# A fused attention and ELU layer on one core: batch 1 turned earlier, the second layer begun earlier, loads moved up

## The chip, the cores and the metric

One core of a Trainium2 chip runs the whole kernel. The metric is the device time in microseconds (us) of one execution; lower is better. Three runs of the kernel before gave 333.58, 333.91 and 334.61 us, with a median of 333.91 us.

## What is computed

```python
# q, k, v: (8 batches, 8 heads, 576 positions, 64), float32
scores = q @ k.T / 8                                   # per batch and head
scores = where(0 <= i - j < 128, scores - slope[h] * |i - j|, -1e9)
attn   = exp(scores - max) / (sum(exp(scores - max)) + 1e-9)
x      = (attn @ v)  laid out as (8 * 576 = 4608 tokens, 8 * 64 = 512)
h      = x @ w_in                                      # 512 -> 2048
g      = where(h > 0, h, exp(min(h, 0)) - 1)           # ELU
out    = g @ w_out                                     # 2048 -> 512, float32
```

A query sees only the 128 positions up to its own, so for each block of 128 keys only 256 queries matter. The 4608 tokens are worked on in nine blocks of 512 by the two layers; a batch has 576 tokens, so token blocks and batches do not line up.

## The kernel before

All matrix work is in float16 on TensorE (PE), with sums in float32 in PSUM. VectorE (DVE), ScalarE (ACT) and GpSimd (POOL) do the rest; POOL also issues the loads. The order of all work is written by hand as a list of slots: in each slot the engines get the pieces below, and each engine runs its own pieces in the order in which they were issued.

The pieces of a slot that matter here:

```python
def hidden(t, c0, w, f0, nf, p):        # first layer: one PSUM bank p of h
    ...                                 # PE: 16 matmuls of 128 columns (32 of 64)
    nc.scalar.activation(e, p, AF.Exp)  # ACT: e = exp(h)
    nc.gpsimd.tensor_scalar(e, e, 1.0, 0.0, min, max)      # POOL

def elu(t, c0, w, f0, nf, p):           # DVE: g = max(e - 1, h); frees the bank p
    V.scalar_tensor_tensor(out=gs[t][...], in0=e, scalar=1.0, in1=p,
                           op0=ALU.subtract, op1=ALU.max)

def output(t, ts, f0, bank=None):       # second layer: 4 of 16 matmuls of 512 columns
    if f0 == 0: ops[t, ts] = bank or ps_o.tile(..., tag="op")
    for fc in range(f0, f0 + 4): nc.tensor.matmul(o, gs[t][...], w_out_sb[...])
    if f0 == 12:
        nc.scalar.copy(ob, o)           # ACT, then SP stores 128 tokens

def values(b, i, part, bank=None):      # attn @ v for four heads of a block of 128 queries
    ...                                 # PE: 4 or 8 matmuls of 65 columns
    V.reciprocal(out=r, in_=a[..., D])  # DVE: rden
    V.tensor_tensor(out=xn, in0=a[..., 0:D], in1=r, op=ALU.mult)    # DVE: xn

def turn(b, i, copy=None, bank=None):   # xn -> xT: 4 PE transposes and a copy, or a DMA

def load_first(b, w, part):             # K (w=1) or Q (w=0) of batch 0 or 1 to SBUF:
    p0, p1 = ((0, 64), (64, 96))[part]  # part 0: positions 0..383, part 1: 384..575
    nc.gpsimd.dma_start(s0[b][p0:p1, w, ...], (q, k)[w][b, :, 6*p0:6*p1, :] ...)

def turn_first(b, w, part, half, bank, copy):   # transposes of that on PE, then one copy
    n, nh = ((64, 2), (32, 4))[part]            # part 0 in two halves of the heads
    for x in range(nh):
        for j in range(6):
            for hh in range(2): nc.tensor.transpose(t[...], s0[b][...], ident[r, r])
    copy(o, t)                                  # PSUM -> QT or KT

def first_scores(b, u, half, d): ...    # PE: q.k of key block u, batches 0 and 1
def first_expo(b, u, half, d, ...): ... # ACT: EX = exp(scores / 8)
def first_weigh(b, u, half): ...        # DVE: EX *= table of slopes and mask
def turn_qk(b, w, h2, dh): ...          # from batch 2 on: K and Q turned on DVE
```

Three banks serve the hidden steps of slots 4 to 17, so the hidden step of slot s can begin only when the `elu` of slot s - 3 has freed its bank:

```python
BUF = [hp[0], hp[1], sp[2], sp[3]]
HID[s if s < 18 else s + 8] = [(*step, BUF[s % 2 if s < 4 else (s + 1) % 3 if s < 18 else (s + 1) % 2])]
...
s = 13 + o if o < 13 else 2 * o + 1 if o < 16 else 17 + o      # slot of second-layer piece o
OUT[s] = (t, ts, 4 * f, sp[3] if t == 0 and ts % 2 else hp[ts - 2] if o >= 16 * NTB - 8 else None)
...
at(6, values, 0, 3, 0); at(6, values, 0, 3, 1, "op")
at(7, turn, 0, 3, nc.scalar.copy)
at(7, values, 0, 4, 0); at(7, values, 0, 4, 1, "op")
at(8, turn, 0, 4, nc.scalar.copy)
```

The loop that issues a slot:

```python
for s in range(min(slots), max(slots) + 1):
    for f, a in early.get(s, []): f(*a)                 # exponentials of earlier scores
    for step in HID.get(s, []): hidden(*step)
    for r in [s - 1] if s < 4 or s > 17 else [] if s == 4 else [s - 2] if s < 17 else [15, 16]:
        for step in HID.get(r, []): elu(*step)
    for f, a in tasks.get(s, []): f(*a)                 # values, turn, scores, loads
    if s in OUT: output(*OUT[s])
```

The first 16 hidden steps are those of token block 0. Slots 18 to 25 have no hidden step: the tokens of the next ones come from batch 1, whose attention is worked out in these slots.

Of the kernel before, what the change touches and what calls it, by code (L numbers as in the profile page):

```python
# [18 lines left out]
def kernel(  # L19
# [9 lines left out]
    nc = tc.nc  # L29
# [4 lines left out]
    NTB = NTOK // 512  # L34
# [3 lines left out]
    V = nc.vector  # L38
# [36 lines left out]
    sp = [spa[:, 0, :], spa[:, 1, :]] + [ps_s.tile([128, 512], F32, name=f"sp{i}", tag=f"sp{i}") for i in (2, 3)]  # L75
    hp = [ps_h.tile([128, 512], F32, name=f"hp{i}", tag=f"hp{i}") for i in range(2)]
# [8 lines left out]
    def load_first(b, w, part):  # L85

        p0, p1 = ((0, 64), (64, 96))[part]
        nc.gpsimd.dma_start(  # L88
            s0[b][p0:p1, w, :, :, :].rearrange("p h j d -> p h (j d)"),
            (q, k)[w][b, :, 6 * p0:6 * p1, :].rearrange("h (p j) d -> p h (j d)", j=6))  # L90
# [8 lines left out]
    def load_v(b, n):  # L99
        p = 128 if n < 4 else 64  # L100
        nc.gpsimd.dma_start(VP[b % 2][0:p, n, :, 0:D],  # L101
                            v[b, :, 128 * n:128 * n + p, :].rearrange("h p d -> p h d"))

    def load_wi(i):
        c = slice(512 * i, 512 * i + 512)
        nc.gpsimd.dma_start(w_in_sb[:, :, c], moe_w_in[:, c].rearrange("(c p) f -> p c f", p=128))
# [31 lines left out]
    with tc.manual_schedule():  # L138
# [104 lines left out]
        def hidden(t, c0, w, f0, nf, p):  # L243
            if p is None:
                p = ps_o.tile([128, 512], F32, name="ho", tag="op")
            hps[t, c0, f0] = p
            a = (512 * t + c0) % RING
            cuts = [(0, w, a)] if a + w <= RING else [(0, RING - a, a), (RING - a, w, 0)]
            for l in range(nf):
                fc = f0 + l  # L250
                for u0, u1, x0 in cuts:
                    for c in range(4):
                        nc.tensor.matmul(  # L253
                            p[:, l * w + u0:l * w + u1], w_in_sb[:, c, fc * 128:(fc + 1) * 128],
                            xT[:, c, x0:x0 + u1 - u0], start=(c == 0), stop=(c == 3))
            e = es[t, c0, f0] = work.tile([128, 512], F32, name="e", tag="e", bufs=6)
            n = w * nf
            nc.scalar.activation(e[:, 0:n], p[:, 0:n], AF.Exp)  # L258
            nc.gpsimd.tensor_scalar(out=e[:, 0:n], in0=e[:, 0:n], scalar1=1.0, scalar2=0.0,  # L259
                                    op0=ALU.min, op1=ALU.max)  # L260

        def elu(t, c0, w, f0, nf, p):
            if t not in gs:
                gs[t] = gpool.tile([128, NFC, 512], F16, name="g", tag="g")
            sh = lambda ap: ap[:, 0:w * nf].rearrange("p (l c) -> p l c", c=w)
            V.scalar_tensor_tensor(  # L266
                out=gs[t][:, f0:f0 + nf, c0:c0 + w], in0=sh(es.pop((t, c0, f0))), scalar=1.0,
                in1=sh(hps.pop((t, c0, f0))), op0=ALU.subtract, op1=ALU.max)

        def output(t, ts, f0, bank=None):  # L270
            if f0 == 0:
                ops[t, ts] = bank if bank is not None else ps_o.tile([128, DO], F32, name="op", tag="op")
            o = ops[t, ts]
            for fc in range(f0, f0 + 4):
                nc.tensor.matmul(o, gs[t][:, fc, ts * 128:(ts + 1) * 128], w_out_sb[:, fc, :],  # L275
                                 start=(fc == 0), stop=(fc == NFC - 1))
            if f0 == 12:
                ob = work.tile([128, DO], F32, name="ob", tag="ob")
                nc.scalar.copy(ob, o)  # L279
                nc.sync.dma_start(out[512 * t + 128 * ts:512 * t + 128 * ts + 128, :], ob)  # L280
# [13 lines left out]
        load_v(0, 0)  # L294
        load_v(0, 1)
        load_first(0, 0, 1)
        load_first(0, 1, 1)
        load_wi(0)
        load_wi(1)
        load_v(0, 2)  # L300
        load_wi(2)
        load_v(0, 3)
# [56 lines left out]
        early, tasks, HID, OUT = {}, {}, {}, {}  # L359

        def at(s, f, *a):
            tasks.setdefault(s, []).append((f, a))

        def before(s, f, *a):
            early.setdefault(s, []).append((f, a))

        BUF = [hp[0], hp[1], sp[2], sp[3]]
# [5 lines left out]
        steps += [(1, 192, 64, 8 * f, 8) for f in range(2)]  # L373
        steps += [(1, c0, 128, 4 * f, 4) for c0 in (256, 384) for f in range(4)]
        for s, step in enumerate(steps):
            HID[s if s < 18 else s + 8] = [(*step, BUF[s % 2 if s < 4 else (s + 1) % 3 if s < 18 else (s + 1) % 2])]
        for t in range(2, NTB):
            for j in range(16):
                step = (128 * (j // 4), 128, 4 * (j % 4), 4) if t < 4 else (256 * (j // 8), 256, 2 * (j % 8), 2)
                HID[16 * t + 8 + j] = [(t, *step, BUF[(j + 1) % 2])]  # L380
        for o in range(16 * NTB):
            t, ts, f = o // 16, o // 4 % 4, o % 4
            s = 13 + o if o < 13 else 2 * o + 1 if o < 16 else 17 + o
            OUT[s] = (t, ts, 4 * f, sp[3] if t == 0 and ts % 2 else hp[ts - 2] if o >= 16 * NTB - 8 else None)


        at(0, values, 0, 1, 0)
# [4 lines left out]
        for half in range(2):  # L392
            at(1, first_scores, 0, 2, half, half)
            for c in range(2):
                before(2 + c, first_expo, 0, 2, half, half, 128 * c, 128 * c + 128)
        at(1, turn_first, 0, 1, 1, 0, None, nc.scalar.copy)
        at(3, values, 0, 2, 0)
        at(3, values, 0, 2, 1, "op")
        at(3, first_scores, 0, 3, 0, 0)
# [15 lines left out]
            at(s, load_wo, 2 + n)  # L415
        at(2, load_first, 1, 1, 0)
        at(3, load_first, 1, 0, 0)
        at(7, load_first, 1, 1, 1)
        at(9, load_first, 1, 0, 1)
        for n, s in enumerate((4, 5, 12, 14, 17)):  # L420
            at(s, load_v, 1, n)
        at(18, turn_first, 1, 1, 0, 0, hp[1], V.tensor_copy)
        at(18, turn_first, 1, 0, 0, 0, sp[2], nc.scalar.copy)
        at(19, turn_first, 1, 1, 0, 1, hp[0], V.tensor_copy)
        at(19, turn_first, 1, 0, 0, 1, "av", nc.scalar.copy)
        at(20, turn_first, 1, 1, 1, 0, sp[2], V.tensor_copy)
        at(21, turn_first, 1, 0, 1, 0, "av", nc.scalar.copy)
        for u, a0, a1, d in ((0, 20, 21, 2), (1, 22, 23, 2), (2, 25, 26, 0), (3, 28, 29, 0)):
            for half, a in enumerate((a0, a1)):
                at(a, first_scores, 1, u, half, d * half)  # L430
                before(a + 1, first_expo, 1, u, half, d * half, 0, 256)
                at(a + 1, first_weigh, 1, u, half)
                at(a + 2, values, 1, u, half, None if half else sp[2])
            at(a1 + 3, turn, 1, u, nc.scalar.copy, sp[3] if u == 0 else sp[2])
        at(31, values, 1, 4, 0, sp[2])
        at(32, values, 1, 4, 1)
        at(33, turn, 1, 4)


        START = [None, None, 35, 49, 65, 83, 100, 118]  # L440
        for b in range(2, B):
            for u in range(4):
                a = START[b] + 4 * u
                at(a, scores, b, u)
                for g in range(4):
                    before(a + 1 + g // 2, expo, b, u, g)
                at(a + 1, weigh, b, u, 0)
                at(a + 2, weigh, b, u, 1)
                at(a + 3, values, b, u, 0)
                at(a + 4, values, b, u, 1)  # L450
                at(a + 4, turn, b, u)
                if u == 3:
                    at(a + 5, values, b, 4, 0)
                    at(a + 6, values, b, 4, 1)
                    at(a + 6, turn, b, 4)
            a = START[b]
            for n in range(4):
                at(a - 8 + n, turn_qk, b, 1, *divmod(n, 2))
                at(a - 4 + n, turn_qk, b, 0, *divmod(n, 2))
                at(a - (17 if b == 2 else 16) + n, load_qk, b, 1, n)  # L460
                at(a - (13 if b == 2 else 12) + n, load_qk, b, 0, n)
            for n in range(5):
                at(a - (9 if b == 2 else 7) + n, load_v, b, n)

        slots = set(HID) | set(OUT) | set(tasks) | set(early)
        for s in range(min(slots), max(slots) + 1):
            for f, a in early.get(s, []):
                f(*a)
            for step in HID.get(s, []):
                hidden(*step)  # L470
            for r in [s - 1] if s < 4 or s > 17 else [] if s == 4 else [s - 2] if s < 17 else [15, 16]:
                for step in HID.get(r, []):
                    elu(*step)
            for f, a in tasks.get(s, []):
                f(*a)
            if s in OUT:
                output(*OUT[s])

# [29 lines left out]
```

The softmax here doesn't subtract the row's maximum and nothing guards it: scores larger than these inputs give would overflow.

## Time and profile before

| | before |
|---|---|
| median of 3 runs | 333.91 us |
| span of the profiled execution | 334.2 us |
| PE busy | 319.1 us (95%) |
| DVE busy | 220.2 us (66%) |
| ACT busy | 183.6 us (55%) |
| POOL busy | 167.0 us (50%) |
| mean granted TensorE clock | 0.988 |

The profile names each group of instructions by its source line: L253 is the matmul of a hidden step, L266 the `elu`, L275 the second layer, L214 and L220/L221 the `values`, L162 the first scores, L126 and L130 the transposes of `turn_first` and their copy, L235/L236 a `turn`. `hp`, `sp`, `spa`, `av` and `op` are PSUM banks. In the table of waits a line reads: who waited, for whom, how long in all, how often, and the longest. In the timeline, the bracket at the end of a line says how long the engine had stood idle and what ended that.

### The profile page before, as it was taken

Reading aid. Unit: us, or ns where it says so; the run is one execution under the profiler, and the core shown is the slowest. Engines: PE = TensorE matmul, PEld = TensorE weight load, DVE = VectorE, ACT = ScalarE, POOL = GpSimd, SP = SyncE. Lnnn points to the kernel's source line nnn. Section 1 sums busy time; section 2 is a strip of 40 time slices with the busy share of each in tenths; the row PEclk is TensorE's granted clock in tenths of the full one; section 3 lists DMA queues with packets and bytes.
Section 4 is the critical chain, followed back from the end, with each engine's and each line's share of the span. In section 5 each row is a group of like instructions: output and inputs, shape, how many; then the busy total and the mean of one; then the engine's idle time right before and its main releaser. Section 6 shows DMA issues by size and latency. Waiting matters only on the chain.

```text
span 334.2 us, 9690 instructions
## 1 busy us (share of the span) xinstructions
PE 319.1 (95%) x4100; PEld 226.4 (68%) x4100; DVE 220.2 (66%) x447; ACT 183.6 (55%) x327; POOL 167.0 (50%) x254
## 2 busy tenths in 40 slices
PE   8988998998999989999999999999999999999995
PEld 7777774576677667777676666666677666666652
DVE  5538542589579776997679767986689666653320
ACT  6666534573655645665665555655554666543421
POOL 8547664084656455645657365735666333323320
PEclk9999996999999999999999999999999999999999
DMA  8999979174899589996999399956979111110011
GB/s 107 197 197 206 185 78 157 51 50 65 104 119 96 74 102 95 98 90 70 122 115 104 83 128 121 95 72 76 136 84 119 42 49 48 49 55 33 31 65 63
DMA packets 93643, 32.02 MB, mean 96 GB/s; under 512 B 81824, under 2 KB 88992, under 8 KB 93600
## 3 DMA queue, kind: packets, MB, share of 16 engines
q0 software_dynamic: 73344, 18.36, 62.5%
q1 hardware_dynamic: 20256, 13.05, 14.8%
q8 instruction: 32, 0.52, 0.6%
q14 instruction: 11, 0.09, 0.1%
HBM read 36.70 MB, written 9.44 MB: 138 GB/s over the span
## 4 chain that ended last, share of the span: by engine, by line
PE 79%; DVE 7%; ACT 3%; DMA 3%; POOL 3%; issue 2%; POOLq 0%; ACTq 0%; DVEq 0%
PE hp L253 32%; PE op L275 31%; PE av L214 4%; PE spa L187 4%; DMA wi<-in_moe_w_in_dram 3%; DVE g L266 3%; PE hp L275 2%; PE sp L275 2%; DVE xn L221 1%; ACT EX L193 1%; ACT e L258 1%; POOL e L259 1%; DVE EX L178 1%; POOL s L88 1%; PE sp L253 1%
## 5 line engine op out<-in xcount | busy, mean ns | idle before, releaser
L259 POOL TENSOR_SCALAR e<-e 128x512 f32<-128x512 f32 x144 | 91.4, 635 | 149.9 <-ACT e L258 148.8
L253 PEld LDWEIGHTS <-wi 128*128 128x128 f16 x1856 | 126.3, 98 | 40.6 <-issue 5.8
L253 PE MATMUL hp<-xT,wi 128*128 128x128 f16 (+2 forms) x1760 | 145.4, 233 | 3.0 <-DVE g L266 1.9
L258 ACT ACTIVATE e<-hp 128x512 f32<-128x512 f32 x139 | 83.6, 602 | 97.7 <-PE hp L253 96.0
L266 DVE SCALAR_TENSOR_TENSOR g<-e,hp 128x512 f16<-128x512 f32 x139 | 93.7, 674 | 64.3 <-POOL e L259 63.5
L275 PE MATMUL op<-wo,g 128*128 128x512 f16 x512 | 132.6, 382 | 0.0
L275 PEld LDWEIGHTS <-g 128*128 128x128 f16 x576 | 50.1, 98 | 44.1 <-issue 7.2
L198 DVE TENSOR_TENSOR EX<-EX,TAB 128x1024 f16<-128x1024 f16 x48 | 33.4, 697 | 8.0 <-ACT EX L193 8.0
L101 POOL DMA_DIRECT2D VP<-in_v_dram x40 | 35.0, 875 | 0.9 <-PE av L214 0.3
L221 DVE TENSOR_TENSOR xn<-av,rden 128x256 f16<-128x256 f32 (+1 forms) x74 | 31.3, 423 | 2.5
L214 PE MATMUL av<-VP,EX 128*128 128x65 f16 x536 | 28.0, 193 | 3.2 <-DVE xn L221 1.6
L214 PEld LDWEIGHTS <-EX 128*128 128x128 f16 x576 | 25.9, 98 | 6.0 <-DVE xn L221 1.8
L279 ACT COPY ob<-op 128x512 f32<-128x512 f32 x32 | 18.7, 585 | 17.8 <-PE op L275 17.8
L193 ACT ACTIVATE EX<-spa 128x512 f16<-128x512 f32 x48 | 26.1, 596 | 4.3 <-PE spa L187 3.8
L193 ACT ACTIVATE EX<-sp 128x512 f16<-128x512 f32 x48 | 26.2, 607 | 0.0
L134 DVE STREAM_TRANSPOSE KT<-st 128x576 f16<-128x576 f16 x24 | 19.7, 821 | 0.0
L134 DVE STREAM_TRANSPOSE QT<-st 128x576 f16<-128x576 f16 x24 | 19.6, 815 | 0.0
L220 DVE RECIPROCAL rden<-av 128x4 f32<-128x4 f32 (+1 forms) x74 | 12.9, 174 | 9.4 <-PE av L214 8.9
L95 POOL DMA_DIRECT2D st<-in_k_dram x24 | 16.4, 683 | 0.1
L95 POOL DMA_DIRECT2D st<-in_q_dram x24 | 16.3, 680 | 0.1
L187 PE MATMUL sp<-QT,KT 32*128 32x256 f16 (+2 forms) x240 | 14.9, 248 | 0.3 <-ACT EX L193 0.2
L187 PE MATMUL spa<-QT,KT 32*128 32x256 f16 (+2 forms) x240 | 14.8, 248 | 0.0
(73 smaller groups left out, 158.8 us busy)
## 6 DMA issues: line engine op xcount, KB each, us to landing
out_dram<-ob SPq DMA_DIRECT2D x36, 256.0 KB, 2.1
VP<-in_v_dram POOLq DMA_DIRECT2D x32, 128.0 KB, 4.2
st<-in_k_dram POOLq DMA_DIRECT2D x24, 144.0 KB, 3.6
st<-in_q_dram POOLq DMA_DIRECT2D x24, 144.0 KB, 4.0
wi<-in_moe_w_in_dram POOLq DMA_DIRECT2D x4, 512.0 KB, 12.0
wo<-in_moe_w_out_dram POOLq DMA_DIRECT2D x4, 512.0 KB, 14.9
s<-in_k_dram POOLq DMA_DIRECT2D x2, 384.0 KB, 8.8
s<-in_q_dram POOLq DMA_DIRECT2D x2, 384.0 KB, 9.9
```

The source lines that it names most:

```text
L101: nc.gpsimd.dma_start(VP[b % 2][0:p, n, :, 0:D], v[b, :, 128 * n:128 * n + p, :].rearrange("h p d -> p h d"))
L134: V.transpose(o, st[b][:, w, h2, n0:n1, :, 32 * dh:32 * dh + 32])
L187: nc.tensor.matmul(sp[g][:, 256 * h2 + o:256 * h2 + o + n], kt_[b % 2][r, k0:k0 + 128], QT[b % 2][r, h2, dh, q0:q0 + n], start=dh == 0, st ...
L193: nc.scalar.activation(unit(b, u)[:, g, :, :], sp[g].rearrange("p (h c) -> p h c", h=2), AF.Exp, scale=0.125)
L198: V.tensor_tensor(out=e, in0=e, in1=TAB[:, int(u == 3), 2 * gp:2 * gp + 2, :, :], op=ALU.mult)
L214: nc.tensor.matmul(a[:, x, h2, :], ex_[u][:, c:c + 128], VP[b % 2][:, n, 2 * g + h2, 0:D + 1], start=j == 0, stop=j == len(parts) - 1)
L221: V.tensor_tensor(out=o, in0=a[0:m, :, :, 0:D], in1=r[0:m].unsqueeze(3).broadcast_to([m, 2, 2, D]), op=ALU.mult)
L253: nc.tensor.matmul(p[:, l * w + u0:l * w + u1], w_in_sb[:, c, fc * 128:(fc + 1) * 128], xT[:, c, x0:x0 + u1 - u0], start=(c == 0), stop=(c ...
L258: nc.scalar.activation(e[:, 0:n], p[:, 0:n], AF.Exp)
L259: nc.gpsimd.tensor_scalar(out=e[:, 0:n], in0=e[:, 0:n], scalar1=1.0, scalar2=0.0, op0=ALU.min, op1=ALU.max)
L266: V.scalar_tensor_tensor(out=gs[t][:, f0:f0 + nf, c0:c0 + w], in0=sh(es.pop((t, c0, f0))), scalar=1.0, in1=sh(hps.pop((t, c0, f0))), op0=A ...
L275: nc.tensor.matmul(o, gs[t][:, fc, ts * 128:(ts + 1) * 128], w_out_sb[:, fc, :], start=(fc == 0), stop=(fc == NFC - 1))
```

## The change

It brings the second layer's first piece from slot 13 to slot 9 (and all its later pieces two slots forward), turns K and Q of batch 1 from slot 16 on instead of slot 18, holds the turns of their last thirds (part 1) back until the first scores have been issued, and so needs only six slots without a hidden step instead of eight. Loads of batch 1 and batch 2 are issued some slots sooner, and the turns of batch 2 on DVE begin three slots sooner against its scores. At the start, one load of K is issued after two loads of `w_in` instead of before them, and one copy moves from ACT to DVE. In slots 3, 6 and 7 the `elu` is issued after the slot's tasks instead of before them. The amount of work of every kind stays the same.

```diff
         load_first(0, 0, 1)
-        load_first(0, 1, 1)
         load_wi(0)
         load_wi(1)
+        load_first(0, 1, 1)
         load_v(0, 2)
...
-            HID[s if s < 18 else s + 8] = [...]
+            HID[s if s < 18 else s + 6] = [...]
...
-                HID[16 * t + 8 + j] = [...]
+                HID[16 * t + 6 + j] = [...]
         for o in range(16 * NTB):
-            s = 13 + o if o < 13 else 2 * o + 1 if o < 16 else 17 + o
-            OUT[s] = (t, ts, 4 * f, sp[3] if t == 0 and ts % 2 else ...)
+            s = (9, 11, 13, 14)[o] if o < 4 else 11 + o if o < 13 else 2 * o - 1 if o < 16 else 15 + o
+            OUT[s] = (t, ts, 4 * f, sp[3] if t == 0 and ts == 2 else ...)
...
-        at(1, turn_first, 0, 1, 1, 0, None, nc.scalar.copy)
+        at(1, turn_first, 0, 1, 1, 0, None, V.tensor_copy)
...
-        at(7, load_first, 1, 1, 1)
-        at(9, load_first, 1, 0, 1)
-        for n, s in enumerate((4, 5, 12, 14, 17)):
+        at(6, load_first, 1, 1, 1)
+        at(7, load_first, 1, 0, 1)
+        for n, s in enumerate((4, 5, 9, 11, 12)):
             at(s, load_v, 1, n)
-        at(18, turn_first, 1, 1, 0, 0, hp[1], V.tensor_copy)
-        at(18, turn_first, 1, 0, 0, 0, sp[2], nc.scalar.copy)
-        at(19, turn_first, 1, 1, 0, 1, hp[0], V.tensor_copy)
-        at(19, turn_first, 1, 0, 0, 1, "av", nc.scalar.copy)
-        at(20, turn_first, 1, 1, 1, 0, sp[2], V.tensor_copy)
-        at(21, turn_first, 1, 0, 1, 0, "av", nc.scalar.copy)
-        for u, a0, a1, d in ((0, 20, 21, 2), (1, 22, 23, 2), (2, 25, 26, 0), (3, 28, 29, 0)):
+        at(16, turn_first, 1, 1, 0, 0, "av", V.tensor_copy)
+        at(16, turn_first, 1, 0, 0, 0, sp[3], nc.scalar.copy)
+        at(17, turn_first, 1, 1, 0, 1, "av", V.tensor_copy)
+        at(17, turn_first, 1, 0, 0, 1, sp[3], nc.scalar.copy)
+        at(19, turn_first, 1, 0, 1, 0, "av", nc.scalar.copy)
+        at(22, turn_first, 1, 1, 1, 0, hp[0], V.tensor_copy)
+        for u, a0, a1, d in ((0, 18, 19, 2), (1, 20, 21, 2), (2, 24, 25, 0), (3, 26, 27, 0)):
             ...                          # scores at a, weigh at a + 1, values at a + 2
-            at(a1 + 3, turn, 1, u, nc.scalar.copy, sp[3] if u == 0 else sp[2])
-        at(31, values, 1, 4, 0, sp[2])   # and 32, 33
+            at(a1 + 3, turn, 1, u, nc.scalar.copy, sp[3] if u else None)
+        at(29, values, 1, 4, 0, sp[2])   # and 30, 31
-        START = [None, None, 35, 49, 65, 83, 100, 118]
+        START = [None, None, 33, 47, 63, 81, 98, 116]
...
-                at(a - 8 + n, turn_qk, b, 1, ...)             # K turned; Q at a - 4 + n
-                at(a - (17 if b == 2 else 16) + n, load_qk, b, 1, n)
+                at(a - (11 if b == 2 else 8) + n, turn_qk, b, 1, ...)   # Q at a - (6 or 4) + n
+                at(a - (20 if b == 2 else 16) + n, load_qk, b, 1, n)
             for n in range(5):
-                at(a - (9 if b == 2 else 7) + n, load_v, b, n)
+                at(a - (12 if b == 2 else 7) + n, load_v, b, n)
...
-            for r in [s - 1] if s < 4 or s > 17 else [] if s == 4 else [s - 2] if s < 17 else [15, 16]:
+            lag = [s - 1] if s < 4 or s > 17 else [] if s == 4 else [s - 2] if s < 17 else [15, 16]
+            late = s in (3, 6, 7)
+            for r in lag if not late else []:
                 for step in HID.get(r, []):
                     elu(*step)
             for f, a in tasks.get(s, []):
                 f(*a)
+            for r in lag if late else []:
+                for step in HID.get(r, []):
+                    elu(*step)
```

## The prediction

> **What bounds the kernel now.** I read the busy times first, then the clock by slices, then what PE waited for, and at last the timeline of the stretches where it waited.
>
> ```profile
> PE 319.1 (95%) x4100; PEld 226.4 (68%) x4100; DVE 220.2 (66%) x447; ACT 183.6 (55%) x327; POOL 167.0 (50%) x254
> ...
> PEclk9999996999999999999999999999999999999999
> ```
>
> PE is busy for 95% of the span, and the change neither adds nor takes away a matmul. So it can only win back PE's waits and the one place where the clock row falls: the seventh slice, a little after 50 us. The chain that ended last is 79% PE, and from 82 us on PE is busy for 245.5 of 252 us. The order of the work there is shifted by two slots as a whole and not otherwise changed, so whatever the change gains or loses must show before about 82 us. PE's waits from 16 to 84 us, by whom they were for (us in total, times, longest):
>
> ```profile
> PE hp L253 <- DVE g L266: 1.7, 4, 0.7
> PE av L214 <- DVE EX L178: 1.1, 2, 0.6
> PE spa L162 <- DVE KT L130: 0.9, 1, 0.9
> PE hp L253 <- DMA wi<-in_moe_w_in_dram: 0.8, 1, 0.8
> PE xps L235 <- DVE xn L221: 0.6, 1, 0.6
> PE spa L162 <- ACT EX L167: 0.5, 1, 0.5
> PE av L214 <- ACT xT L236: 0.5, 1, 0.5
> ```
>
> All of these together are some 6 us, under 2% of the time. Now the clock, by stretches of 3.41 us around the fall (columns: stretch, its length, busy us of PE, PEld, DVE, ACT, POOL, then the clock, the DMA share and GB/s):
>
> ```profile
> 29.36:32.78 3.42, 2.71 (x55) 2.33 (x53) 2.87 (x10) 1.55 (x3) 2.95 (x5) 1.00 1.24 207
> ...
> 46.43:49.84 3.41, 3.41 (x104) 2.15 (x102) 1.97 (x4) 1.35 (x2) 2.65 (x5) 1.00 0.45 93
> 49.84:53.26 3.42, 2.51 (x63) 1.45 (x58) 1.67 (x2) 0.80 (x1) 3.42 (x6) 1.00 1.29 123
> 53.26:60.08 6.82, 6.82 (x70) 3.05 (x69) 1.85 (x4) 3.78 (x6) 0.48 (x1) 0.50 1.30 155
> ```
>
> From 53.26 to 60.08 us PE ran at half clock while it had work all the time: 6.82 us for what full clock does in 3.4. Before that it had stood idle for 0.9 us, and had spent 0.83 us on transposes (L126), so that only some 1.3 us of 3.4 were true matmuls.
>
> **What the Trainium skill says.** The page "TensorE: Matmul & The Clock Gate", section "Part 1: The HAM clock gate", says that a monitor looks at windows of about 3.4 us and halves the clock after an idle one. The trace agrees in the length (6.82 us are two windows) and the 0.50, but here the window was far from idle. The same page, "Part 4: PE-mode transpose", says that transposes don't count as busy in the same way. The trace fits that, weakly: the window from 46.43 is full, half of it transposes, and was followed by no fall at once. The same page, under "Architectural detail", says that VectorE takes its work strictly in order. Here the trace agrees: in the timeline below each `g` comes exactly where the program has it.
>
> **The change, part by part.** H7 is the hidden step of slot 7, and so on; found in PE's timeline by counting groups of 16 matmuls. A hidden step costs 0.89 us of PE when one follows another (34.72 to 35.62), a second-layer piece 0.86 to 0.97, a turn of 48 transposes 0.83.
>
> *First load.* H1 waited 0.80 us for `wi`, to 17.84. With 192 KB of K out of its way it lands about a microsecond sooner (estimate: DMA moves about 0.2 MB per us there). Gain 0.8.
>
> *The copy of KT in slot 1 on DVE, and slot 3's late `elu`.* The copy takes 0.96 us on DVE and now stands ahead of `g` of slot 1, for which H3 must wait, so H3 gains nothing (about 22.6 instead of 22.44). But ACT loses a copy of 0.80 us, so the exponentials come earlier (the 0.5 goes), and in slot 3 `xn` no longer stands behind a `g` (the 0.6 goes). H5 comes at about 26.05 instead of 27.24: gain 1.2, with the first load in it.
>
> *Late `elu` in slots 6 and 7.* This is the part that I hold against the change. In the timeline of before, DVE (first lines) and PE (last lines):
>
> ```profile
> 29.16 0.68 DVE L266 SCALAR_TENSOR_TENSOR g<-e,sp 128x512 f16<-128x512 f32 x1
> 29.75 0.17 DVE L220 RECIPROCAL rden<-av 128x4 f32<-128x4 f32 x1
> ...
> 30.51 0.42 DVE L221 TENSOR_TENSOR xn<-av,rden 128x256 f16<-128x256 f32 x1
> 30.85 0.68 DVE L266 SCALAR_TENSOR_TENSOR g<-e,hp 128x512 f16<-128x512 f32 x1
> ```
>
> ```profile
> 29.04 0.67 PE L214 MATMUL av<-VP,EX 128*128 128x65 f16 x16
> 29.89 1.07 PE L253 MATMUL sp<-xT,wi 128*128 128x128 f16 x16 [0.18 <-DVE g L266]
> 30.99 0.40 PE L235 MATMUL xps<-ident,xn 128*128 128x128 f16 x4
> ...
> 32.36 1.06 PE L253 MATMUL hp<-xT,wi 128*128 128x128 f16 x16
> ```
>
> H7 needs the bank that the `g` at 29.16 frees, and today starts 0.85 us after `values` (29.04). Issued after the tasks, this `g` stands behind both `rden` and `xn` of those values. From slot 0, where the same five follow one another, values to end of `g` take 2.24 us (16.38 to 18.62). So H7 starts 2.29 us after values: 1.44 later, and 0.1 for `values` itself, which catches up with its weights. In slot 7 the second half of `values` ends 2.47 us after H7 starts (32.36 less 29.89); then 0.2 to `rden`, about 0.6 to the end of `xn`, 0.67 for `g`: H8 starts 3.94 after H7 instead of 2.47, another 1.47. H9 gets back about 0.3. Cost 2.7. At H9 the changed kernel is then 1.5 behind (2.7 less 1.2).
>
> *Second layer from slot 9.* H9 to H13 took 4.36 us (33.83 to 38.19) where four steps need 3.56; the chain ACT, POOL, DVE behind three banks sets that. With two pieces of output between them PE has other work. Gain 0.8; 0.7 behind at slot 13.
>
> *Turns from slot 16, last thirds held back.* The wait of 0.9 for KT goes, since the scores that it held up now come before that copy. The turns now lie between hidden steps and outputs, so I take no half clock here: gain 3.3 (half of 6.82, little of it beside other waits). New waits: in slot 18 ACT copies an output (0.58) ahead of the exponential, so slot 20's values wait about 0.6; slot 21's about 0.5; in slot 22 the KT copy (0.96) stands on DVE ahead of the second weighing, and slot 23's values wait about 1.15, where before there was 0.6. Net: 0.9 + 3.3 - 1.6 = 2.6 gained.
>
> *Batch 2 sooner.* The four turns of K on DVE (0.82 each) move out of a stretch where DVE was busy for 3.9 of 4 us, but into one that the above has filled. Walking slots 24 to 31 with the rows' durations I get waits of about 2.0 where there were 1.8. Cost 0.2.
>
> Sum: +0.7 - 2.6 + 0.2 = -1.7, or 332.2 us.
>
> **Rivals.** *The half clock moves forward.* With the late `elu`, PE would have about 5.7 us, from 28.5 to 34.2, with only 1.6 us of work. That is emptier than the window that brought the fall (1.3 of 3.4, with turns beside it). If the monitor acts on such a window, 6.8 us at half clock follow, less what falls into waits: about 3 us back, and 335.2. Against it: one fall does not give the threshold, and the window's place against the stretch is chance. I give it 6 in 10. *The late `elu` costs little*, since what looks like a wait is made up at once by earlier `xn`, and the outputs from slot 9 fill in: then 329.5. Against it stands that nothing but that `g` frees H7's bank. 15 in 100. *The turns still bring the fall*, as 192 transposes still lie within 10 us: 3.3 back, 335.5, or 338 with both falls; 12 in 100. *Loads collide*: POOL now issues loads of K for batch 2 in slots 13 to 16 beside its own steps of 0.61; three banks give it 5 us for a chain of 3.2, so I expect nothing.
>
> **Range and chances.** The two main cases are 332.2 and 335.2; weighed with the others the middle is 333.4. Each wait that I worked out may be off by half a microsecond, so 8 times in 10 it should lie from 329.5 to 336.5. For 2% it would have to gain or lose 6.7 us; more than all the waits named, if the half clock doesn't go as well, so faster 0.05, slower 0.03.
>
> **What would show it.** In the profile after: the wait for `wi` gone and H5 about 1.2 us earlier; waits of about 1.6 us before H7 and before H8, both ended by `g`, L266; no wait for KT of 0.9 in the first scores of batch 1; the clock row whole in the seventh slice, and either a fall in the fifth or none; small waits of `values` for EX around 55 to 62 us. If H7 and H8 don't wait, or the clock falls nowhere and the waits are still there, the sum or the main rival is wrong. A time under 329.5 would mean that the late `elu` is harmless.

## The result, and the profile after

| | before | after |
|---|---|---|
| median of 4 runs each | 334.0 us | 334.44 us |
| lowest and highest | 333.58, 334.61 | 334.17, 334.51 |
| PE busy in the profiled execution | 319.1 us | 316.1 us |
| mean granted TensorE clock there | 0.988 | 1.000 |

The ratio is 1.001 with a 95% interval of 0.9993 to 1.0028: no difference. The experiments brought more executions of both kernels: a median of 334.6 us over 150 of the kernel before, 334.5 over 18 of the changed one.

The busy times and the clock row of the page after, the same two lines that the prediction showed of before:

```profile
PE 316.1 (95%) x4100; PEld 225.2 (68%) x4100; DVE 221.5 (67%) x448; ACT 183.4 (55%) x326; POOL 166.4 (50%) x254
...
PEclk9999999999999999999999999999999999999999
```

The clock doesn't fall, and PE is busy for 3 us less with the same matmuls; that is about what 6.82 us at half clock had added before (half of it, 3.4). What PE waited for from 16 to 84 us (us in total, times, longest):

```profile
PE hp L253 <- DVE g L266: 2.7, 3, 1.3
PE av L214 <- DVE EX L178: 1.6, 3, 0.8
PE sp L253 <- DVE g L266: 1.6, 1, 1.6
PE av L214 <- ACT xT L236: 0.7, 1, 0.7
PE spa L162 <- ACT EX L167: 0.6, 1, 0.6
PE hp L253 <- DMA wi<-in_moe_w_in_dram: 0.4, 1, 0.4
PE sp L214 <- DVE EX L178: 0.2, 1, 0.2
```

The waits for KT (0.9) and for `xn` (0.6) are gone; that for `wi` is halved (in a second profile of the same kernel, a_again below, it is gone too). But hidden steps now wait 4.3 us for `g` where it was 1.9. Two of these waits make up 2.9 us. In the timeline (DVE first, then PE) they are those of H7 and H8:

```profile
29.40 0.42 DVE L221 TENSOR_TENSOR xn<-av,rden 128x256 f16<-128x256 f32 x1
...
29.74 0.68 DVE L266 SCALAR_TENSOR_TENSOR g<-e,sp 128x512 f16<-128x512 f32 x1
```

```profile
28.19 0.65 PE L214 MATMUL av<-VP,EX 128*128 128x65 f16 x16
30.48 1.07 PE L253 MATMUL sp<-xT,wi 128*128 128x128 f16 x16 [1.64 <-DVE g L266]
31.38 0.39 PE L235 MATMUL xps<-ident,xn 128*128 128x128 f16 x4
...
34.42 1.05 PE L253 MATMUL hp<-xT,wi 128*128 128x128 f16 x16 [1.31 <-DVE g L266]
```

H7 starts 2.29 us after the values (28.19 to 30.48), H8 3.94 us after H7 (30.48 to 34.42). In the kernel before it was 0.85 and 2.47. The `g` that frees H7's bank begins only when the last `xn` of slot 6 is through.

### The profile page after: what moved, and what is told of

It reads as the page before. It is cut to its first block, busy times and chain, and to the rows that moved or that the text cites. A ratio compares the mean times of both kernels' runs of the same rounds, so it can differ in the third digit from the quotient of the medians.

```text
span 332.7 us, 9682 instructions
## 1 busy us (share of the span) xinstructions
PE 316.1 (95%) x4100; PEld 225.2 (68%) x4100; DVE 221.5 (67%) x448; ACT 183.4 (55%) x326; POOL 166.4 (50%) x254
## 4 chain that ended last, share of the span: by engine, by line
PE 79%; DVE 6%; DMA 5%; POOL 3%; ACT 3%; issue 2%; POOLq 0%; ACTq 0%
PE hp L253 34%; PE op L275 32%; PE av L214 5%; PE spa L187 4%; DMA wi<-in_moe_w_in_dram 3%; PE hp L275 2%; DVE g L266 2%; DMA VP<-in_v_dram 2%; PE sp L253 1%; DVE xn L221 1%; ACT EX L193 1%; POOL VP L101 1%; ACT e L258 1%; DVE EX L198 1%; POOL e L259 1%
## 5 line engine op out<-in xcount | busy, mean ns | idle before, releaser
L275 PE MATMUL op<-wo,g 128*128 128x512 f16 x528 | 135.6, 379 | 0.0
L275 PEld LDWEIGHTS <-g 128*128 128x128 f16 x576 | 49.8, 97 | 43.0 <-issue 5.5
```

## Where the time went, stage by stage

To compare the stages without the clock I use the kernel before with the fall prevented (run b_warm20 below), and the distance from one hidden step's first matmul to another's, read from the traces. H18 is the first hidden step after batch 1's slots. From the changed kernel's stages the work that it has moved into them is taken off (two output pieces are 1.72 us, one group of scores 0.33).

| stage | before, clock whole | after | work moved | gain (-) or loss | predicted |
|---|---|---|---|---|---|
| H0 to H5 | 11.56 | 10.72 | 0 | -0.8 | -1.2 |
| H5 to H9 | 6.60 | 9.26 | 0 | +2.7 | +2.7 |
| H9 to H13 | 4.35 | 5.31 | -1.72 | -0.8 | -0.8 |
| H13 to H18 | 24.91 | 22.14 | +1.72 + 0.33 | -0.7 | +0.7 without the clock |
| H18 to H26 | 16.60 | 17.45 | -0.33 | +0.5 | +0.2 |

The sum is +0.9. With the clock whole the executions say the same: a median of 333.7 us before and 334.5 after, +0.8. The clock then gives this back, as the next section shows. The first row is the least sure: the second profile of the changed kernel (a_again) has 10.48 us there, which makes it -1.1 and the sum +0.6, while its other rows agree within 0.05. Likewise the kernel before took 11.76 us from H0 to H5 in its own profile.

## The experiments

Each kernel ran beside the kernel before on one chip. "Whole" below is the median of those executions whose mean granted clock was over 0.9965, so that no window at half clock lies in the work; the others, called falls, are given apart. (A mean of 0.997 still counts as whole: the clock also falls after the last matmul, in a_again at 331.2 us where PE ends at 329.0.) This split is needed because the kernel before itself has three levels: of its 150 executions 63 were whole (median 333.7 us), 46 had a mean clock of 0.992 or 0.993 (334.8) and 41 one of 0.988 to 0.990 (336.1). The profiled execution of before, with 0.988 and 6.82 us at half clock, belongs to the last group. In the middle group the mean stands for 4.7 to 5.3 us at half clock; one window of 3.4 us in the work and the rest after the last matmul would make that, but none of this group was profiled.

**a_late3: the late elu in slot 3 alone**

```diff
-            late = s in (3, 6, 7)
+            late = s == 3
```

> The changed kernel with the late elu in slot 3 alone; in slots 6 and 7 the elu is issued before the tasks again. If the late elu is what ate the gain, the waits of 1.6 us before H7 and 1.3 us before H8 go and the time falls by 2.0 to 3.0 us against the changed kernel, to about 332. If the time was not lost there but the half clock of the kernel before was never part of its usual runs (the rival), those waits still go, but PE meets other waits soon after and the time falls by under 1 us.

Measured: 332.57 us over 13 executions, whole 332.5 (12 of them); ratio to the kernel before 0.9934 (0.9908 to 0.9959). That is 2.0 us below the changed kernel's whole 334.5, against 2.7 worked out for slots 6 and 7. PE's waits, three lines of the same view:

```profile
PE hp L253 <- DVE g L266: 1.6, 3, 0.8
PE sp L126 <- issue: 0.7, 1, 0.7
...
PE sp L253 <- DVE g L266: 0.2, 1, 0.2
```

The waits of 1.6 and 1.3 are gone. At H17 the kernel is 2.9 us ahead of the changed one; at H18 it is 2.1 ahead. A new wait of 0.7 in the transposes of slot 17, for nothing that the profile names, takes most of that difference.

**b_late367: the kernel before with the late elu alone**

```diff
-            for r in [s - 1] if s < 4 or s > 17 else [] if s == 4 else ...:
+            lag = [s - 1] if s < 4 or s > 17 else [] if s == 4 else ...
+            late = s in (3, 6, 7)
+            for r in lag if not late else []:
                 ...                      # elu
             ...                          # the slot's tasks
+            for r in lag if late else []:
+                ...                      # elu
```

> The kernel before with nothing changed but the late elu in slots 3, 6 and 7. If the late elu costs what the trace of the changed kernel shows, the time rises by 2 to 3 us less what slot 3 gives (0.5 to 1), so to about 336. If the waits are made up at once, it stays within 0.7 us of the kernel before. With a stretch as empty as this the clock may fall a second time near 35 us; then it rises by 5 us or more.

Measured: 337.08 us over 22 executions, ratio 1.0086 (1.0061 to 1.0111). Whole 336.0 (7 executions): +2.3 on 333.7. The other 15 took 336.7 to 339.8. Some of these falls are the kernel before's own; but nine have a mean clock of 0.995 or 0.983, which none of the 150 has. In its profiled execution the clock fell, by windows:

```profile
29.15:32.56 3.41, 1.77 (x40) 1.65 (x38) 1.86 (x6) 0.63 (x2) 2.12 (x3) 1.00 1.24 207
32.56:35.98 3.42, 1.41 (x30) 1.22 (x28) 2.44 (x7) 1.05 (x2) 1.17 (x2) 1.00 1.27 203
35.98:39.39 3.41, 3.41 (x36) 3.12 (x33) 1.22 (x2) 1.35 (x3) 0.61 (x1) 0.50 1.75 184
```

PE was busy for 1.77 and 1.41 us of two windows of 3.4 us, and then ran for one window at half clock. So the late `elu` costs twice: the wait itself, and a clock that can fall after it.

**b_warm20: a wait filled**

```diff
         at(20, turn_first, 1, 1, 1, 0, sp[2], V.tensor_copy)
+        at(20, warm, 16)          # 16 matmuls on the identity, result unused
```

> The kernel before with 16 spare matmuls of 128 columns (0.9 us, their result unused) between the turns of K and the scores of slot 20, where PE otherwise waits 0.9 us for the copy of KT. If the wait beside the transposes is what halves the clock at 53 us, the clock stays whole; in runs that had the fall this is worth up to 3.3 us, and the median falls by as much as the fall is common. If transposes or the mix as a whole bring the fall, it stays and the time is the same within 0.5 us.

Measured: 333.83 us over 22 executions, from 333.44 to 334.12, ratio 0.9973 (0.9958 to 0.9987). Not one had a fall; of the kernel before's 58 executions on the same chip 26 had one. The 192 transposes are still there, so they alone don't bring the fall; the wait of 0.9 us beside them is needed. Whether the transposes are needed too, no run shows. And with the clock whole this is what the kernel before takes when its own clock is whole (333.7): the fall is worth 1.1 us in the one group, 2.4 in the other, and not 3.3 in all of them.

**a_ktact: the copy of KT in slot 1 back on ACT**

```diff
-        at(1, turn_first, 0, 1, 1, 0, None, V.tensor_copy)
+        at(1, turn_first, 0, 1, 1, 0, None, nc.scalar.copy)
```

> The changed kernel with the copy of KT in slot 1 back on ACT. By the prediction this copy on DVE makes H3 wait 0.65 us (seen) but frees ACT for exponentials, so that the two cancel to within 0.5 us. If the copy on DVE is a loss, the time falls by 0.6 us or more; if ACT is what bounds slots 2 to 4, it rises by about 0.5.

Measured: whole 334.7 (11 of 14 executions), 0.2 above the changed kernel; all 14, 334.86. From H0 to H5 it needs 10.70 us, the changed kernel 10.72 in its first profile and 10.48 in its second. So the copy's place on DVE is worth 0.2 us at most: what H3 waits, the exponentials win.

**a_again: the changed kernel once more**

> The changed kernel itself again, for more of its executions, to see whether its clock ever falls. The empty stretch before H7 and H8 (1.9 of 5.7 us of work) should bring a fall near 35 us in some of them, as it did in the kernel before with the late elu; by the rival the earlier arrival of PE and the outputs behind it keep the clock whole. Median 334.4 if whole, 335.5 or more in executions with a fall.

Measured: 334.66 us over 14 executions; whole 334.5 (11), and three of 335.7 to 335.9 with a clock of 0.992. With the first four that makes 3 falls in 18. Where they lie isn't known, since the profiled execution had none. Its windows were as thin as those above, though; of the changed kernel's first profile:

```profile
29.34:32.76 3.42, 1.59 (x30) 1.50 (x31) 1.64 (x5) 1.07 (x2) 2.03 (x4) 1.00 1.24 206
32.76:36.17 3.41, 2.10 (x38) 1.85 (x38) 2.38 (x5) 0.66 (x2) 0.67 (x2) 1.00 1.29 204
36.17:39.58 3.41, 3.41 (x48) 2.73 (x46) 1.38 (x2) 1.59 (x4) 2.50 (x4) 1.00 1.88 179
```

1.59 of 3.42 us brought no fall; 1.41 did in b_late367, and 1.55 in a_out13 below. The thin stretch is there: the emptiest 3.41 us of it, wherever a window might begin, hold 1.40 us of PE in this profile (from 31.60 us) as in b_late367's (from 32.00). In b_late367 a window lay nearly there. Here, and in a_again (1.81 and 1.85 us), the windows cut the stretch in two. That the fall depends on how the windows lie fits this, but isn't shown.

**a_out13: the second layer's first pieces back in slot 13**

```diff
-            if s in OUT:
-                output(*OUT[s])
+            for o in {9: [], 11: [], 13: [9, 11, 13]}.get(s, [s]):
+                if o in OUT:
+                    output(*OUT[o])
```

> The changed kernel with the second layer's first two pieces back in slot 13 (three pieces there), so that slots 9 to 12 have hidden steps alone again. By the prediction these two pieces filled waits of 0.8 us: the time rises by 0.8 us, with waits of H10 to H13 for g back in the trace. If they filled nothing, or the later pieces make it up, the time is the same within 0.3 us.

Measured: 335.92 us over 20 executions; whole 335.7 (11), 1.2 above the changed kernel. H12 and H13's waits for `g` are back (0.3 and 0.5 in the timeline of the profiled execution, where the clock was whole again). The other 9 had a fall; in the profiled one it lies from 34.83 to 38.24:

```profile
31.41:34.83 3.42, 1.55 (x33) 1.36 (x31) 1.69 (x5) 1.07 (x2) 1.25 (x3) 1.00 1.25 204
34.83:38.24 3.41, 3.27 (x32) 2.98 (x32) 1.32 (x4) 0.86 (x2) 0.61 (x1) 0.50 1.43 196
```

So the early pieces are worth 1.2 us, more than the 0.8 predicted. Falls were also more frequent without them, 9 in 20 against 3 in 18, which is little to go by.

**a_kt22act: the last copy of KT on ACT**

```diff
-        at(22, turn_first, 1, 1, 1, 0, hp[0], V.tensor_copy)
+        at(22, turn_first, 1, 1, 1, 0, hp[0], nc.scalar.copy)
```

> The changed kernel with the last copy of KT (slot 22) on ACT, which is idle there, instead of DVE. The wait of 1.2 us in slot 23 for the weighing falls to about 0.3, and if nothing is given back later, the time falls by 0.9 us. If DVE is the bound of slots 22 to 31 as a whole, it falls as much, since 0.96 us of DVE work leaves the stretch. If PE's later waits in slots 25 to 31 have other ends (the rival), under 0.4 us.

Measured: whole 334.23 (10 of 14 executions), 0.25 below the changed kernel's 334.48; all 14, 334.3. The longest wait of `values` for EX falls from 0.8 to 0.5:

```profile
PE av L214 <- DVE EX L178: 1.3, 3, 0.5
```

From H17 to H18 it gains 0.4 us, and H18 to H26 stays as it was (17.44 us against 17.45). The rival was right: the other waits of the stretch have other ends.

**a_b2old: the turns of batch 2 at their old distance**

```diff
-                at(a - (11 if b == 2 else 8) + n, turn_qk, b, 1, *divmod(n, 2))
-                at(a - (6 if b == 2 else 4) + n, turn_qk, b, 0, *divmod(n, 2))
+                at(a - 8 + n, turn_qk, b, 1, *divmod(n, 2))
+                at(a - 4 + n, turn_qk, b, 0, *divmod(n, 2))
```

> The changed kernel with the turns of batch 2 on DVE at their old distance from their scores (K 8 and Q 4 slots ahead instead of 11 and 6); loads as changed. By the prediction the new place costs 0.2 us, so the time is the same within 0.4 us, with the waits of slots 22 to 25 smaller and those of slots 25 to 31 larger. If DVE is too full in slots 22 to 25, the time falls by 0.6 or more; if the move was a gain, it rises by as much.

Measured: whole 334.75 (10 of 14), 0.3 above the changed kernel; all 14, 335.06. H18 to H26 takes 17.75 us instead of 17.45. The earlier turns are a gain of 0.3, not a cost of 0.2. What makes H18 to H26 longer than in the kernel before all the same (17.45 against 16.60, with 0.33 of moved work) stays open.

**b_start: the kernel before with the start of the change**

```diff
-        load_first(0, 1, 1)
         load_wi(0)
         load_wi(1)
+        load_first(0, 1, 1)
...
-        at(1, turn_first, 0, 1, 1, 0, None, nc.scalar.copy)
+        at(1, turn_first, 0, 1, 1, 0, None, V.tensor_copy)
...
+            late = s == 3             # and the loop as changed
```

> The kernel before with the changes at its start alone: wi loaded ahead of the second load of K, the copy of KT in slot 1 on DVE, and the late elu in slot 3. By the prediction H5 comes 1.2 us earlier; the trace of the changed kernel shows 0.9. With the clock whole 332.7 us against 333.7. If the gain is given back at the waits of H7 and H9 that follow, under 0.3 us. Falls of the clock at slot 20 stay as common as in the kernel before.

Measured: whole 333.0 (15 of 22), 0.7 below the kernel before; all 22, 333.25, ratio 0.9964 (0.9947 to 0.998). Nothing is given back at H7 and H9: H5 to H9 takes 6.59 us against 6.60. Falls were not as common as expected: 7 of 22, where the kernel before had 27 of 43 on this chip. Why is open, since the turns stand where they stood.

**a_nolate: no late elu at all**

```diff
-            late = s in (3, 6, 7)
+            late = False
```

> The changed kernel with no late elu at all, in slot 3 neither. If the late elu pays in slot 3, where no hidden step waits for the bank that it holds, this is 0.3 to 0.7 us above the variant with the late elu in slot 3 alone (332.5). If it pays nowhere, it is the same within 0.2 us.

Measured: 332.14 us over 6 executions, none with a fall, ratio 0.9918 (0.9888 to 0.9948). It is not above a_late3 (332.5) but at or below it, and from H0 to H5 both need 10.48 us. The late `elu` pays in slot 3 neither.

**c1 and c2: the change mended**

```diff
-            late = s in (3, 6, 7)
+            late = s == 3
...
-        at(1, turn_first, 0, 1, 1, 0, None, V.tensor_copy)
+        at(2, turn_first, 0, 1, 1, 0, None, V.tensor_copy)
...
-        at(22, turn_first, 1, 1, 1, 0, hp[0], V.tensor_copy)
+        at(22, turn_first, 1, 1, 1, 0, hp[0], nc.scalar.copy)
```

> The changed kernel with the late elu in slot 3 alone, the last copy of KT (slot 22) on ACT, and the turn of batch 0's last third of K moved from slot 1 to slot 2, behind the g of slot 1 on DVE. From 332.5: the wait of H3 (0.65) goes and 0.25 comes from the copy on ACT, so 331.7 with the clock whole; 332.3 or more if these are given back in the stretch from 60 to 80 us, which DVE bounds.

Measured: 332.16 us over 22 executions, whole 332.0 (18; the other four took 334.2 to 337.2), ratio 0.9925 (0.9906 to 0.9945). The wait of H3 is gone: H1 to H3 takes 5.03 us instead of 5.42 (a_again: 5.66) in the changed kernel, with the same work. But a longer wait stands in the transposes of slot 17:

```profile
PE sp L126 <- issue: 1.8, 1, 1.8
```

c2 adds this:

```diff
-                nc.scalar.copy(ob, o)
+                (V.tensor_copy if (t, ts) == (0, 1) else nc.scalar.copy)(ob, o)
```

> As the run before it (c1), and the copy of the output of tokens 128 to 255 in slot 18 on DVE, idle there, instead of ACT, where it stood 0.58 us ahead of the first exponential of batch 1. The waits of values in slots 20 and 21 (0.5 us each) should go: 0.5 to 0.9 us below c1. If DVE, which has to take these 0.6 us, bounds the stretch that follows, nothing is won.

Measured: 331.59 us over 6 executions, whole 331.3 (5) and one of 336.7 with a clock of 0.985; ratio 0.9901 (0.9865 to 0.9937), without that one. It is the fastest of the study by its median, about 1% below both kernels, but over six executions only. The gain over c1 can't be credited to the copy alone, since the wait in slot 17 was 1.0 us in c2's profile and 1.8 in c1's.

## Why the prediction was right, and where it was not

The time lies in the range, 1.0 us above the point, and "within 2%" was given 0.92. The main mechanism is shown, but two of the steps were off (the half clock and the turns), and part of that cancelled, so that the point came so close is in part luck.

*The late elu in slots 6 and 7.* Right in mechanism and size. Worked out: H7 1.44 later after values, H8 1.47 later after H7, 0.3 back at H9. Measured: 1.44 (2.29 less 0.85), 1.47 (3.94 less 2.47), and 0.27 (1.47 less 1.20 from H8 to H9). Taking it out again gave 2.0 us of the 2.7. The rival that it would cost little has fallen.

*The half clock goes.* This step failed in size. The prediction took 3.3 us as gained, from one profile. That profile was of an execution with two windows at half clock; such were 41 of 150, and 63 had no fall at all. In the median the fall costs the kernel before 0.9 us (334.6 less 333.7), and even two windows cost only 2.4. Why 6.82 us at half clock cost 2.4 and not 3.4 is shown in part, beside b_warm20 with its whole clock: the 48 transposes of slot 21 took 1.39 us instead of 0.86 (54.81 to 56.20 and 53.87 to 54.73), not twice as long, and a wait of 0.18 us for EX is gone. The rest stays open. That the turns' new place ends this fall fits the profile, the 18 executions, and the variants without the late `elu` in slots 6 and 7 (a_late3, a_nolate, c1, c2: 6 falls in 47 executions, against 87 in 150 before), but no run moved the turns alone.

*The fall moves forward.* Given 6 in 10 and 3 us. At most 3 of 18 executions had it, at 1.3 us each (335.8 against 334.5), and 11 of 42 of the variants that leave the stretch as it is (a_ktact, a_kt22act, a_b2old); the place of these falls isn't known. The stretch itself came nearly as worked out: from 28.84 to 34.42 us PE was busy for 1.94 of 5.58 us. That such a stretch can bring a fall is shown by b_late367 and a_out13, where it lies at 36 and 35 us. Why the changed kernel, whose stretch is as thin, has it more rarely stays open; that the outputs from slot 9, which refill PE sooner, are a part of it isn't shown.

*Turns from slot 16.* Predicted a loss of 0.7 apart from the clock (0.9 won, 1.6 of new waits), measured a gain of 0.7. The waits in slots 20 and 21, worked out as 0.6 and 0.5, are 0.18 and under 0.1 us in the timeline; slot 23's is 0.84 instead of 1.15. ACT did copy the output ahead of the exponential for slot 20, as foreseen (53.25 and 53.73), but the values that wait for it had their turn only at 55.4.

*First load, KT copy, slot 3.* Predicted -1.2, measured -0.8 and -1.1 in the stages of the two profiles and -0.7 in b_start's time. The wait for `wi` was halved in one profile and gone in the other. The late `elu` in slot 3 was counted as part of the gain and has none.

*Second layer from slot 9.* Predicted -0.8; -0.8 in the stages, 1.2 when taken out. *Batch 2 sooner.* Predicted +0.2; taken out, it is 0.3 better than the old place.

*Readings.* Three figures of the prediction don't come out of its own lines. The window before the fall held 1.5 us of matmuls other than transposes (2.51 less 1.02 on L126), not 1.3. The wait that slot 23's is set against was 0.47 us in the profile of before (at 63.93), not 0.6. And weighed by the chances given, its cases come to 333.6 to 334.1, by how they overlap, not to 333.4.

In sum: +0.8 with the clock whole, and 0.9 less in the median for falls that became rare: the same time.

## What to carry to other kernels

An instruction moved back in one engine's queue delays everything behind it: before moving it, ask which buffer it frees and who waits for that buffer next. Here the result of `xn` was wanted soon, but the `g` in front of it held the bank that PE needed first. And one profile is one execution: where the clock falls in some executions and not in others, look at the clock of all of them before a fall is put into the sum.

## What the runs showed of the hardware

- The fall of the clock came in whole windows: 6.82 us in the profile of before, 3.41 us in b_late367 and a_out13. The Trainium skill, "TensorE: Matmul & The Clock Gate", section "Part 1: The HAM clock gate", says that the clock halves after an idle window of about 3.4 us and that these windows are free-running. These runs agree in the length and in that the fall differs by execution. But none of the windows before a fall was idle: ones with PE 41% and 45% busy (1.41 and 1.55 of 3.42 us) were enough, while 46% (1.59 of 3.42) was not. These numbers are no threshold: in before the fall followed a window with 2.51 us busy, 1.02 of it transposes, while in b_late367 none followed one with 2.92 us, 1.81 of it transposes (53.04 to 56.46). Whether transposes count or not, the busy share of the window before doesn't put all five in order.
- 0.9 us of spare matmuls in a wait, which cost nothing measurable, kept the clock whole in 22 of 22 executions.
- In the quicker variants PE stands still inside a group of transposes in slot 17, for 0.3 us (a_nolate) to 1.8 us (c1), with no semaphore to wait for. In all four profiles that have it (a_late3, a_nolate, c1, c2) PE stops at the same instruction, behind 11 of 24 transposes, and goes on 2.3 to 2.5 us after a load of 16 KB of instructions began (c1: load at 47.4, stand from 48.0 to 49.8). The 48 transposes of a slot are 96 instructions, with their weight loads, in 0.9 us. In the changed kernel's first profile this load began at 46.6 us, PE came to the place at about 50.6, and there is no stand. That PE ran out of instructions is only argued from this; no run tried it, and it may be the next bound here.
